# Retention and mixture of experts on one core: later pairs' q loaded by heads, GpSimd's scalings and the early counts reordered

## The chip, the cores and the metric

The kernel runs on one core of a Trainium2 chip. Five engines work side by side, each with an instruction queue of its own that it executes in order: TensorE (PE; its weight loads are listed apart, as PEld), VectorE (DVE), ScalarE (ACT), GpSimd (POOL) and SyncE (SP), which here only issues DMAs. They meet at semaphores. Data moves between HBM and the on-chip memory over 16 DMA engines that all queues share. TensorE writes into PSUM, eight banks of 2 KB in each of 128 partitions.

The metric is the device time of one execution in microseconds. The time before is 455.89 us, the median of three runs (453.74 to 457.38).

## The reference

Two blocks follow each other. The first is retention with a decay for each head, for 4 batches, 8 heads, 768 tokens and a head size of 64:

```python
gamma = 1.0 - 2.0 ** (-5.0 - np.arange(H, dtype=np.float32))
...
for t in range(S):
    state = gamma[None, :, None, None] * state + np.einsum('bhd,bhe->bhde', k[:, :, t], v[:, :, t])
    y[:, :, t] = scale * np.einsum('bhd,bhde->bhe', q[:, :, t], state)
```

Its output, as 3072 rows of 512, goes through a layer of 8 experts. Each row goes to the one expert with the largest logit:

```python
logits = x @ w_gate
expert_idx = np.argmax(logits, axis=1)
...
    h = np.maximum(x_sorted[lo:hi] @ w1[e], 0.0)
    y_sorted[lo:hi] = h @ w2[e]
...
return (gate_w[:, None] * y).astype(np.float32)
```

w1 is 8 x 512 x 1024 and w2 is 8 x 1024 x 512, all in float32.

## The kernel before

**Retention in chunks.** The tokens of a batch are cut into six chunks of 128. A step `s` (0 to 11, `STEPS` is 12) handles one chunk of two batches: `where[s]` gives `m` (which 256 tokens), `b1` (which two batches) and `e` (which half of the 256). Two steps in a row, an even and an odd one, make a pair: they share one load of q, 256 tokens of two batches. Decays are folded into q and v by a table, `dec`: q is multiplied by a forward decay (`scale_q`, giving `qs`), v by a backward one (`scale_v`, giving `vs`), and the products then need no decay of their own.

In a step, TensorE computes in this order: `scores` (k against q, line 532), `with_state` (the old state against q, 555), the gate's logits of the step before (614, 623), the transposes of the next step's k (`turn_k`, 500), in odd steps the transposes of the next pair's q (`turn_q`, 500), the new state (`next_state`, 568) and `within` (masked scores against vs, 586). VectorE masks the scores (`am`, 536), adds the state (574) and turns the outputs to rows (`to_rows`, 597). ScalarE copies transposes out of PSUM (`qT`, 513; `kT`, 519) and the outputs (589, 592). SyncE issues the loads of q three steps ahead, of k three ahead and of v two ahead, and stores the rows to `x_d` in HBM, four DMAs a step (604). GpSimd does the scalings (489, 494).

**q before the change.** For each batch of a pair one DMA brings 256 tokens of all heads, two tokens to a partition, into a tile of its own (four buffers). `scale_q(s, b)` scales batch `b`: two instructions, one for the even and one for the odd tokens. `turn_q(s, b)` transposes these and two ScalarE copies interleave them into `qT2[b]`.

**Order of the work.** All five queues are written out by hand (`manual_schedule`), in the order of the loop at line 788. For GpSimd that is, in step `s`: `scale_q(s+1, 1)` if `s` is odd, then the `scale_v` that `SCALED` names (the step's own by default), then `scale_q(s+2, 0)` if `s` is even. `SCALED` gives step 8 the v of steps 8 and 9, step 9 that of step 10, and step 10 none.

**Routing beside it.** `place(i)` is a generator with the routing of steps 0 to 4, 5 to 8 and 9 to 11 (`NEXT`). `WHEN` says at which points of which steps its next portion is put into the queues. `place(1)` starts in step 9; its last portion, in step 10 after the logits' transposes, is `found` (708), `inv` (712), `sources` (184 to 187) and the gathers of the first 256 rows of experts 0 and 1, with the `scale_v` of step 11 between. It leaves a count per expert in `acc[:, 2]`. `pad_ranks` (725 to 731) then raises the counts of these two experts, so that later rows don't fill places of the gathered 256: a small matmul `tot` and three VectorE instructions. It is called in step 10 after `next_state`. `found`, `tot`, the new state and the transposes of k all take banks of the PSUM tag "tr", which has two.

**Experts.** While the last step still runs, the 256 gathered rows of expert 0 go through w1 (`hp`, 232) and w2; then the experts follow one by one, with products split in quarters and halves (311, 357) and plain ones for the rest (245). The tiles `we` reuse the bytes of q's tiles.

Of the kernel before, what the change touches and what calls it, by code (L numbers as in the profile page):

```python
# [13 lines left out]
F32 = mybir.dt.float32  # L14
# [4 lines left out]
ALU = mybir.AluOpType  # L19
AX = mybir.AxisListType  # L20

P = 128


NC = 6


def decay_table(H, D):

    gamma = 1.0 - 2.0 ** (-5.0 - np.arange(H, dtype=np.float64))
    i = np.arange(P, dtype=np.float64)[:, None]
    on = [gamma ** (2 * P * m + 2 * i + e + 1) / math.sqrt(D) for m in range(NC // 2) for e in range(2)]
    back = [gamma ** -(P * c + i + 1) for c in range(NC)]
    return np.concatenate(on + back, 1).astype(np.float32)


def inner(ap, n):

    dims = [list(d) for d in ap.ap]
    return bass.AP(tensor=ap.tensor, offset=ap.offset, ap=dims + [[0, n]])
# [9 lines left out]
def kernel(  # L54
# [11 lines left out]
    nc = tc.nc  # L66
    B, H, S, D = q.shape
# [3 lines left out]
    HP = H // 2  # L71
# [24 lines left out]
    x_d = dram.tile([N, Q * DT * L], F32, tag="x_d", name="x_d")  # L96


    dec = const.tile([P, 2 * NC * H], F32, tag="dec", name="dec")
    wg = const.tile([P, DT, P // DT], F32, tag="wg", name="wg")  # L100
    ident = const.tile([P, P], F32, tag="ident", name="ident")
    ones = const.tile([P, P], F32, tag="ones", name="ones")
# [39 lines left out]
    acc = rt([P, NR + 1, E], "acc", BF16)  # L142
# [112 lines left out]
    FH, DH = FT // 2, DM // 2  # L255
# [195 lines left out]
    with ExitStack() as actx:  # L451
        att = actx.enter_context(tc.tile_pool(name="att", bufs=2))
# [13 lines left out]
        where = [(s // 4, s // 2 % 2, s % 2) for s in range(STEPS)]  # L466
        raw, front, state, x = {}, {}, {}, {}
        lg = keep.tile([P, NT, E], F32, tag="lg", name="lg")
        qT2 = [None, None]

        def load(nm, s, b, parts=1):
            m, b1, e = where[s]
            src = {"q": q, "k": k, "v": v}[nm]
            if nm == "q":
                to = att.tile([P, H, 2 * D], F32, tag=nm, name=nm, bufs=4)
                for part in (ts(i, H // parts) for i in range(parts)):
                    nc.sync.dma_start(to[:, part, :], src[2 * b1 + b, part, ts(m, 2 * P), :].rearrange(
                        "h (t e) d -> t h (e d)", e=2))
            else:
                to = att.tile([P, H, D], F32, tag=nm, name=nm, bufs=8)  # L480
                nc.sync.dma_start(to, src[2 * b1 + b, :, ts(2 * m + e, P), :].rearrange("h t d -> t h d"))
            raw[nm, s, b] = to

        def scale_q(s, b, by=nc.gpsimd, parts=1):
            got = raw.pop(("q", s, b))
            qs = raw["qs", s, b] = att.tile([P, 2, H, D], F32, tag="qs", name="qs")
            for part in (ts(i, H // parts) for i in range(parts)):
                for e in range(2):
                    by.tensor_tensor(out=qs[:, e, part, :], in0=got[:, part, ts(e, D)], op=ALU.mult,  # L489
                                     in1=inner(dec[:, ts(2 * where[s][0] + e, H)][:, part], D))  # L490

        def scale_v(s, b, by=nc.gpsimd):
            vs = att.tile([P, H, D], F32, tag="vs", name="vs", bufs=4)
            by.tensor_tensor(out=vs, in0=raw.pop(("v", s, b)), op=ALU.mult,  # L494
                             in1=inner(dec[:, ts(NC + 2 * where[s][0] + where[s][2], H)], D))
            raw["vs", s, b] = vs

        def heads_first(src, tr, pairs=range(HP)):
# [5 lines left out]

        def turn_q(s, b, parts=1, by=(nc.scalar.copy, nc.scalar.copy)):
            qs = raw.pop(("qs", s, b))
            qT2[b] = att.tile([P, HP, P, 2], F32, tag="qT", name="qT")
            trs = [pairs_of("sc", 4, "trq") for _ in range(2)]
            for i in range(parts):
                for e in range(2):  # L510
                    heads_first(qs[:, e, :, :], trs[e], range(i * HP // parts, (i + 1) * HP // parts))
            for e in range(2):
                by[e](out=qT2[b][:, :, :, e], in_=trs[e])

        def turn_k(s, b):
            kT = att.tile([P, HP, P], F32, tag="kT", name="kT")
# [3 lines left out]
            front[s, b] = kT  # L520

        def q_of(s, b):
            return qT2[b][:, :, ts(where[s][2], P // 2), :].rearrange("p a t e -> p a (t e)")

        def scores(s, b):
            kT, qT = front.pop((s, b)), q_of(s, b)
# [103 lines left out]
        def place(i):  # L630
# [82 lines left out]
            if i == NR - 2:  # L713
                head = inv[:, :, 0 : TC + HALF]
                src, far = sources(head, "_e")
                for e in range(2):
                    gather(xs2[e], src[:, e * TC :], range(HALF), 2 * NEXT[i + 1] * P)
                    if e == 0:
                        for b in range(2):
                            scale_v(STEPS - 1, b)  # L720
                early.extend([head, far])

        def pad_ranks(at):

            tot = ps("tr", 2, "tot")[:, 0:2]
            nc.tensor.matmul(tot, lhsT=ones_b, rhs=at, start=True, stop=True)
            pad = att.tile([P, 2], F32, tag="pad", name="pad")
            nc.vector.scalar_tensor_tensor(out=pad, in0=inner(row2[:, 0], 2), scalar=float(EARLY), in1=tot,
                                           op0=ALU.add, op1=ALU.subtract)
            nc.vector.tensor_scalar(out=pad, in0=pad, scalar1=0.0, scalar2=2.0, op0=ALU.max, op1=ALU.min)  # L730
            nc.vector.tensor_tensor(out=at, in0=at, in1=pad, op=ALU.add)
# [45 lines left out]
                copies[t](out=xT[:, :, ts(t, P)], in_=tr)  # L777

        VALUES = {STEPS - 5: (STEPS - 3, STEPS - 2)}
        SCALED = {STEPS - 4: (STEPS - 4, STEPS - 3), STEPS - 3: (STEPS - 2,), STEPS - 2: ()}  # L780
        rest = iter(())
        WHEN = {5: "abc", 6: "b", 7: "ab", 8: "pp", 9: "ac", 10: "mpp"}

# [4 lines left out]
        for s in range(STEPS):  # L788
            if s + 3 < STEPS:
                if s % 2:  # L790
                    load_all("q", s + 3)
                load_all("k", s + 3)
            for i in VALUES.get(s, (s + 2,) if s + 5 < STEPS else ()):
                load_all("v", i)
            if s % 2 and s + 1 < STEPS:
                scale_q(s + 1, 1)
            for i in SCALED.get(s, (s,) if 0 < s < STEPS - 1 else ()):
                for b in range(2):
                    scale_v(i, b)
# [24 lines left out]
            if s:  # L824
                if s + 1 < STEPS:
                    logit = logits(s - 1)
                    ahead()
                if s + 1 == STEPS:
                    xe = whole_rows(xs2[0])
                reduce = logits_of(s - 1, *logit)  # L830
                step(s, "p")
                if s + 1 < STEPS:
                    ahead_q()
                to_rows(s - 1)
                reduce()
# [12 lines left out]
            step(s, "b")  # L848
            if s == NEXT[NR - 1] + 1:
                pad_ranks(acc[:, NR - 1, 0:2])  # L850
            step(s, "r")
            within(s, y, am, (lambda: early_rows(xe, xTa, (nc.vector.tensor_copy, nc.scalar.copy)))
                   if s + 1 == STEPS else lambda: None)
            step(s, "c")
# [1 line left out]
        egates, edst = gates_of(early[0], "_e"), targets(*early, "_e")  # L856
        rest = place(NR - 1)
        oa = xs2[0][:, 0:HALF, :]
        we = [att.tile([P, FH * DH], F32, tag=tag, name="we", bufs=bufs)
              for tag, bufs in [("q", 4)] * 4]  # L860


        def within_early(f):
# [260 lines left out]
```

## Time and profile before

| | |
|---|---|
| median of three runs | 455.89 us |
| the profiled execution's own time | 458.76 us |
| its span, first to last instruction | 456.8 us |
| busy: PE, PEld, DVE, ACT, POOL | 430.3, 361.4, 292.1, 131.9, 260.5 us |
| mean granted clock of TensorE | 0.987 |
| share of the chain that ended last: PE, DMA, DVE | 75%, 7%, 7% |
| DMA share over the first 12 of 40 slices | 0.8 to 0.9 or more |
| DMA packets, bytes | 94471, 72.75 MB |

The span is what the profiler saw of the engines; about 2.0 us lie around it in the execution's own time. Retention takes about the first 126 us, the experts the rest. A busy TensorE is not TensorE at its peak: matmuls are pipelined and their ends are modelled. Three groups of the page belong to the change:

| group | count | mean ns |
|---|---|---|
| POOL qs (489), 128x512 | 22 | 1042 |
| POOL vs (494), 128x512 | 23 | 1045 |
| SyncE loads of q (477), 512 KB | 11 | lands 6.1 us after issue |

In a view's line, "idle before <- releaser" in square brackets is the time for which the engine had stood still and what ended that wait.

### The profile page before, as it was taken

The page shows a single profiled execution, that of the slowest core. Times are in us where ns is not written, and L with a number is a line of the kernel's source. Part 1 is how long each engine was busy: PE and PEld are TensorE (multiplying, and loading weights), DVE is VectorE, ACT ScalarE, POOL GpSimd, SP SyncE. Part 2 cuts the span into 40 slices and gives each one's busy share as a digit, 9 for nine tenths or more (in the row PEclk, how much of TensorE's full clock was granted, in tenths as well). Part 3 has the DMA queues.
Part 4 walks back from the last instruction along what each step waited for, and adds up shares of the span by engine and source line. Part 5 has one row for each costly group of instructions (what it writes and reads, how often), then busy time and mean ns, then how long its engine had stood idle before and what let it go on. Part 6 is the DMA issues. An engine that isn't in the chain of part 4 may idle for free.

```text
span 456.8 us, 9680 instructions
## 1 busy us (share of the span) xinstructions
PE 430.3 (94%) x3651; PEld 361.4 (79%) x3651; DVE 292.1 (64%) x600; ACT 131.9 (29%) x298; POOL 260.5 (57%) x216
## 2 busy tenths in 40 slices
PE   6999998969799999999999999999899999999992
PEld 3788887858678868869968985997798689599772
DVE  4454787667868974775776678387677768744410
ACT  2356354334342112310331321124133113202310
POOL 4474544252506978519845890985489189278311
PEclk9999999989899999999999999999999999999997
DMA  8999999999966546644532815172272534001001
GB/s 190 213 236 205 229 205 219 238 214 250 304 187 230 187 120 218 250 187 128 192 99 94 279 53 183 42 292 85 110 249 74 187 101 164 6 5 64 4 29 50
DMA packets 94471, 72.75 MB, mean 159 GB/s; under 512 B 53898, under 2 KB 78474, under 8 KB 94352
## 3 DMA queue, kind: packets, MB, share of 16 engines
q1 hardware_dynamic: 89088, 58.74, 45.9%
q0 software_dynamic: 5120, 12.60, 8.2%
q8 instruction: 47, 0.77, 0.7%
q14 instruction: 72, 0.59, 0.4%
q10 hardware_dynamic: 144, 0.05, 0.0%
HBM read 60.88 MB, written 14.68 MB: 165 GB/s over the span
## 4 chain that ended last, share of the span: by engine, by line
PE 75%; DMA 7%; DVE 7%; issue 4%; SPq 3%; POOL 2%; ACT 1%; POOLq 0%; ACTq 0%; DVEq 0%
PE p L311 27%; PE p L357 17%; PE p L245 13%; DMA q<-in_q_dram 4%; PE hp L232 3%; PE y L586 3%; DMA v<-in_v_dram 3%; SPq L604 2%; PE sc L532 2%; PE p L232 2%; PE new L568 1%; PE y L555 1%; DMA w1t<-in_moe_w_dram 1%; PE yp L357 1%; POOL qs L489 1%
## 5 line engine op out<-in xcount | busy, mean ns | idle before, releaser
L245 PE MATMUL p<-w2t,hT 128*8 128x128 f32 (+6 forms) x496 | 66.4, 360 | 0.0
L245 PEld LDWEIGHTS p<-w2t,hT 128*8 128x8 f32 (+6 forms) x496 | 32.6, 123 | 29.2 <-issue 26.4
L405 POOL DMA_INDIRECT out_dram<-o,dst x30 | 29.9, 995 | 29.1 <-ACT o L253 13.0
L216 DVE STREAM_TRANSPOSE xT<-xs 32x512 f32<-32x512 f32 (+1 forms) x64 | 40.7, 635 | 6.8 <-issue 5.5
L536 DVE TENSOR_TENSOR am<-sc,causal 128x512 f32<-128x512 f32 x48 | 30.0, 683 | 21.0 <-PE sc L532 20.9
L494 POOL TENSOR_TENSOR vs<-v,dec 128x512 f32<-128x512 f32 x23 | 23.7, 1045 | 33.5 <-DMA v<-in_v_dram 33.3
L311 PE MATMUL p<-t,s 128*128 128x196 f32 (+5 forms) x224 | 41.7, 329 | 0.0
L311 PE MATMUL p<-t,w1t 128*128 128x196 f32 (+5 forms) x224 | 41.7, 329 | 0.0
L1083 POOL COPY turn_of<-t 128x1 f32<-128x1 f32 x6 | 1.1, 184 | 70.1 <-DVE t L297 70.1
L315 DVE TENSOR_TENSOR hT<-p,q 128x196 f32<-128x196 f32 (+5 forms) x84 | 28.6, 359 | 16.6 <-PE p L311 16.0
L216 DVE STREAM_TRANSPOSE xTs<-xs 32x512 f32<-32x512 f32 x48 | 33.7, 702 | 7.0 <-issue 6.1
L173 POOL DMA_INDIRECT xs<-x_d,src x28 | 29.6, 1059 | 14.8 <-issue 8.0
L311 PEld LDWEIGHTS p<-t,s 128*128 128x128 f32 x224 | 37.8, 190 | 0.0
L311 PEld LDWEIGHTS p<-t,w1t 128*128 128x128 f32 x224 | 37.8, 190 | 0.0
L357 PE MATMUL p<-ws,hs 128*128 128x256 f32 x168 | 37.4, 379 | 0.0
L315 DVE TENSOR_TENSOR q<-p,q 128x196 f32<-128x196 f32 (+5 forms) x56 | 19.0, 360 | 26.8 <-ACT q L323 13.5
L357 PEld LDWEIGHTS p<-ws,hs 128*128 128x128 f32 x168 | 31.9, 190 | 4.3
L273 POOL TENSOR_TENSOR ws<-w2t,ws 128x1024 f32<-128x1024 f32 x14 | 34.4, 2455 | 0.6
L273 POOL TENSOR_TENSOR ws<-w2t 128x1024 f32<-128x1024 f32 x14 | 33.2, 2369 | 0.1
L489 POOL TENSOR_TENSOR qs<-q,dec 128x512 f32<-128x512 f32 x22 | 22.3, 1042 | 17.0 <-DMA q<-in_q_dram 16.1
L363 DVE SCALAR_TENSOR_TENSOR o<-p,gate,q 128x256 f32<-128x256 f32 x21 | 10.0, 483 | 27.9 <-PE p L357 23.8
L357 PE MATMUL p<-w2t,hT 128*128 128x256 f32 x112 | 26.9, 381 | 0.1
(203 smaller groups left out, 835.1 us busy)
## 6 DMA issues: line engine op xcount, KB each, us to landing
w1t<-in_moe_w_dram SPq DMA_DIRECT2D x7, 2048.0 KB, 8.7
w2t<-in_moe_w_dram SPq DMA_DIRECT2D x7, 2048.0 KB, 9.4
k<-in_k_dram SPq DMA_DIRECT2D x24, 256.0 KB, 5.1
v<-in_v_dram SPq DMA_DIRECT2D x24, 256.0 KB, 5.7
x_d<-xg SPq DMA_DIRECT2D x48, 128.0 KB, 3.9
q<-in_q_dram SPq DMA_DIRECT2D x11, 512.0 KB, 6.1
w1t<-in_moe_w_dram SPq DMA_DIRECT2D x2, 1024.0 KB, 8.6
w2t<-in_moe_w_dram SPq DMA_DIRECT2D x2, 1024.0 KB, 9.8
```

The source lines that it names most:

```text
L173: nc.gpsimd.indirect_dma_start(out=xs[:, t, :], out_offset=None, in_=x_d[0:rows, :], in_offset=bass.IndirectOffsetOnAxis(ap=idx[:, t : t + ...
L216: nc.vector.transpose(xT[ts(g, L), :, 0 : n * P].rearrange("p a (t r i) -> p r t a i", r=Q, i=L)[:, r, :, :, :], xs[ts(r, L), tiles[0] : t ...
L232: nc.tensor.matmul(hp, lhsT=w1t[:, 0, dt, ts(f, P)], rhs=xT[:, dt, 0:n], start=(dt == 0), stop=(dt == DT - 1))
L245: nc.tensor.matmul(y[j * z : j * z + m, 0:c], lhsT=hT[:, f, t * P + r0 : t * P + r0 + m], rhs=w2t[:, 0, f, ts(j, c)], start=(i == 0), stop ...
L273: by.tensor_tensor(out=ws[i], in0=sums[i][0], in1=sums[i][1], op=ALU.subtract)
L311: nc.tensor.matmul(rows(y), lhsT=a(d, f), rhs=b(d), start=start and d == 0, stop=d == 1, skip_group_check=True)
L315: nc.vector.tensor_tensor(out=to, in0=rows(y), in1=rows(plus), op=ALU.add)
L357: nc.tensor.matmul(y, lhsT=a[:, f, :], rhs=b[:, f, :], start=start and f == 0, stop=f == FH - 1, skip_group_check=True)
L405: done = nc.gpsimd.indirect_dma_start(out=out[:, :], out_offset=bass.IndirectOffsetOnAxis(ap=idx[:, t : t + 1], axis=0), in_=o[:, t, :], i ...
L489: by.tensor_tensor(out=qs[:, e, part, :], in0=got[:, part, ts(e, D)], op=ALU.mult, in1=inner(dec[:, ts(2 * where[s][0] + e, H)][:, part], D))
L494: by.tensor_tensor(out=vs, in0=raw.pop(("v", s, b)), op=ALU.mult, in1=inner(dec[:, ts(NC + 2 * where[s][0] + where[s][2], H)], D))
L536: nc.vector.tensor_tensor(out=am[j], in0=sc[j], in1=middle(causal[:, :], HP), op=ALU.mult)
```

## The change

Four things change. First, from the second pair on, q comes by heads: one DMA per head brings the 256 tokens of both batches, four tokens (1024 B) to a partition, and the partitions alternate between the batches. The tile holds the pair, so there are two buffers of twice the size. The first pair keeps its layout inside the new tile. The decay table gets columns for the four tokens. Second, `scale_q(s, b)` and `turn_q(s, b)` with `b` 0 and 1 now stand for tokens 0, 1 and 2, 3 of each four, of both batches; ScalarE's copies put them in place in one tile `qT` for both batches. Third, `SCALED` leaves step 8 its own v alone and gives step 9 the v of steps 9 and 10. Fourth, `pad_ranks` moves from step 10 after `next_state` into the last portion of `place(1)`, behind the gathers.

```diff
+R = 4
+ON = 2 + R * NC // 2
...
-    on = [gamma ** (2 * P * m + 2 * i + e + 1) / math.sqrt(D) for m in range(NC // 2) for e in range(2)]
+    on = [gamma ** (2 * i + e + 1) / math.sqrt(D) for e in range(2)]
+    on += [gamma ** (2 * P * m + R * (i // 2) + r + 1) / math.sqrt(D) for m in range(NC // 2) for r in range(R)]
...
-    dec = const.tile([P, 2 * NC * H], F32, tag="dec", name="dec")
+    dec = const.tile([P, (ON + NC) * H], F32, tag="dec", name="dec")
...
             if nm == "q":
-                to = att.tile([P, H, 2 * D], F32, tag=nm, name=nm, bufs=4)
+                if (nm, s) not in raw:
+                    raw[nm, s] = att.tile([P, H, R * D], F32, tag=nm, name=nm, bufs=2)
+                if s:
+                    for h in range(b * H // 2, (b + 1) * H // 2):
+                        nc.sync.dma_start(raw[nm, s][:, h, :],
+                                          src[2 * b1 : 2 * b1 + 2, h, ts(m, 2 * P), :].rearrange(
+                                              "b (i r) d -> i b (r d)", r=R))
+                    return
                 for part in (ts(i, H // parts) for i in range(parts)):
-                    nc.sync.dma_start(to[:, part, :], src[2 * b1 + b, part, ts(m, 2 * P), :].rearrange(
+                    nc.sync.dma_start(raw[nm, s][:, part, ts(b, 2 * D)], src[2 * b1 + b, part, ts(m, 2 * P), :].rearrange(
                         "h (t e) d -> t h (e d)", e=2))
...
         def scale_q(s, b, by=nc.gpsimd, parts=1):
-            got = raw.pop(("q", s, b))
+            got = raw["q", s]
+            on = 2 + R * where[s][0] + 2 * b if s else 0
...
-                    by.tensor_tensor(out=qs[:, e, part, :], in0=got[:, part, ts(e, D)], op=ALU.mult,
-                                     in1=inner(dec[:, ts(2 * where[s][0] + e, H)][:, part], D))
+                    by.tensor_tensor(out=qs[:, e, part, :], in0=got[:, part, ts(2 * b + e, D)], op=ALU.mult,
+                                     in1=inner(dec[:, ts(on + e, H)][:, part], D))
...
-            qT2[b] = att.tile([P, HP, P, 2], F32, tag="qT", name="qT")
+            if b == 0:
+                qT2[0] = att.tile([P, HP, 2, 2 * P], F32, tag="qT", name="qT", bufs=1)
...
-                by[e](out=qT2[b][:, :, :, e], in_=trs[e])
+                if s:
+                    by[e](out=qT2[0].rearrange("p a b (i r) -> p a i b r", r=R)[:, :, :, :, 2 * b + e],
+                          in_=trs[e].rearrange("p a (i b) -> p a i b", b=2))
+                else:
+                    by[e](out=qT2[0][:, :, b, :].rearrange("p a (t e) -> p a t e", e=2)[:, :, :, e], in_=trs[e])
...
-            return qT2[b][:, :, ts(where[s][2], P // 2), :].rearrange("p a t e -> p a (t e)")
+            return qT2[0][:, :, b, ts(where[s][2], P)]
...
                         for b in range(2):
                             scale_v(STEPS - 1, b)
+                pad_ranks(acc[:, NR - 1, 0:2])
                 early.extend([head, far])
...
-        SCALED = {STEPS - 4: (STEPS - 4, STEPS - 3), STEPS - 3: (STEPS - 2,), STEPS - 2: ()}
+        SCALED = {STEPS - 3: (STEPS - 3, STEPS - 2), STEPS - 2: ()}
...
             step(s, "b")
-            if s == NEXT[NR - 1] + 1:
-                pad_ranks(acc[:, NR - 1, 0:2])
             step(s, "r")
...
-        we = [att.tile([P, FH * DH], F32, tag=tag, name="we", bufs=bufs)
-              for tag, bufs in [("q", 4)] * 4]
+        we = [x[:, i, :] for x in (att.tile([P, 2, FH * DH], F32, tag="q", name="we", bufs=2) for _ in range(2))
+              for i in range(2)]
```

More of the change, by code (lines that the diff above doesn't have):

```diff
@@ L468 @@
         lg = keep.tile([P, NT, E], F32, tag="lg", name="lg")
-        qT2 = [None, None]
+        qT2 = [None]
         def load(nm, s, b, parts=1):
@@ L474, in load @@
             if nm == "q":
[L475 removed]
+                if (nm, s) not in raw:
[6 more added lines that the diff above has]
+                    return
                 for part in (ts(i, H // parts) for i in range(parts)):
[L477 removed]
+                    nc.sync.dma_start(raw[nm, s][:, part, ts(b, 2 * D)], src[2 * b1 + b, part, ts(m, 2 * P), :].rearrange(
                         "h (t e) d -> t h (e d)", e=2))
             else:
[L480 removed]
+                to = raw[nm, s, b] = att.tile([P, H, D], F32, tag=nm, name=nm, bufs=8)
                 nc.sync.dma_start(to, src[2 * b1 + b, :, ts(2 * m + e, P), :].rearrange("h t d -> t h d"))
[L482 removed]
         def scale_q(s, b, by=nc.gpsimd, parts=1):
[L485 removed]
+            got = raw["q", s]
+            on = 2 + R * where[s][0] + 2 * b if s else 0
             qs = raw["qs", s, b] = att.tile([P, 2, H, D], F32, tag="qs", name="qs")
@@ L494, in scale_v @@
             by.tensor_tensor(out=vs, in0=raw.pop(("v", s, b)), op=ALU.mult,
-                             in1=inner(dec[:, ts(NC + 2 * where[s][0] + where[s][2], H)], D))
+                             in1=inner(dec[:, ts(ON + 2 * where[s][0] + where[s][2], H)], D))
             raw["vs", s, b] = vs
```

## The prediction

> **What bounds the kernel now.** I read the granted clock first, then the chain of waits, then each engine's timeline where the chain leaves TensorE. From 126 us on, the chain is almost only TensorE and what feeds it from inside the chip: a microsecond won before 126 is a microsecond at the end. Ahead of 126 the chain alternates between loads (q, v), GpSimd's scalings and TensorE. The change acts in that part alone. Two holes stand out there. In this view of stretches the columns after the stretch are its length, then busy time of PE, PEld, DVE, ACT, POOL, then granted clock, DMA share and GB/s:
>
> ```profile
> 96.30:99.80 3.50, 0.06 (x2) 0.02 (x1) 3.24 (x6) 0.55 (x2) 3.15 (x4) 1.00 0.97 233
> 100.10:103.50 3.40, 3.26 (x16) 2.29 (x13) 0.71 (x1) 1.83 (x3) 3.40 (x4) 0.50 0.94 224
> ...
> 117.10:119.50 2.40, 0.00 (x1) 0.01 (x1) 2.40 (x3) 0.00 (x0) 2.24 (x3) 1.00 0.89 262
> 120.60:124.00 3.40, 3.40 (x42) 2.52 (x34) 2.01 (x4) 1.08 (x3) 0.68 (x1) 0.50 0.93 277
> ```
>
> TensorE stands still for 3.5 and for 2.4 us, and after each hole its clock is 0.50 for 3.4 us. The timeline (start, length) says who makes the first hole:
>
> ```profile
> 96.65 2.08 POOL L494 TENSOR_TENSOR vs<-v,dec 128x512 f32<-128x512 f32 x2 [10.24 <-DMA v<-in_v_dram]
> ...
> 98.69 4.05 POOL L489 TENSOR_TENSOR qs<-q,dec 128x512 f32<-128x512 f32 x4
> ...
> 99.78 3.99 PE L500 MATMUL trq<-ident,qs 128*128 128x128 f32 x16 [3.44 <-POOL qs L489]
> ...
> 100.10 0.71 DVE L648 TENSOR_TENSOR ohs<-em,idx 128x64 bf16<-128x64 f32 x1
> ...
> 103.70 1.97 PE L586 MATMUL y<-am,vs 128*64 128x128 f32 x32
> ...
> 105.94 1.27 PE L532 MATMUL sc<-qT,kT 64*128 64x128 f32 x18
> ```
>
> GpSimd, in order, sits 10.24 us on v of step 9; q of step 10 landed at 89.8 and 91.7 (packet and semaphore records) and is scaled only afterwards, so TensorE's transposes `trq` wait and then go at GpSimd's pace. The second hole:
>
> ```profile
> 112.69 0.32 DVE L712 TENSOR_TENSOR inv<-inv,found 128x160 f32<-128x160 f32 x1
> ...
> 113.06 0.16 PE L726 MATMUL tot<-acc,ones_b 128*128 128x2 bf16 x1
> ...
> 114.11 1.25 POOL L173 DMA_INDIRECT xs<-x_d,src_e  x1 [7.44 <-DMA w1t<-in_moe_w_dram]
> ...
> 116.17 2.61 DVE L731 TENSOR_TENSOR acc<-acc,pad 128x2 bf16<-128x2 bf16 x1
> 116.69 2.05 POOL L494 TENSOR_TENSOR vs<-v,dec 128x512 f32<-128x512 f32 x2
> ...
> 118.70 2.47 DVE L536 TENSOR_TENSOR am<-sc,causal 128x512 f32<-128x512 f32 x4
> ...
> 119.52 0.64 PE L614 MATMUL parts<-xT,wg 128*32 128x256 f32 x8 [2.42 <-DVE am L536]
> ```
>
> A two-element addition of `pad_ranks` takes 2.61 us and ends with GpSimd's two `vs`; a like one of eight elements (L678) takes 0.17 us at 106.74, with no scaling beside it. The mask `am` and TensorE wait behind it. Finally the load queue, from the timeline of SyncE:
>
> ```profile
> 84.57 2.08 SPq L477 DMA_DIRECT2D q<-in_q_dram  x2
> ...
> 100.51 6.42 SPq L604 DMA_DIRECT2D x_d<-xg  x8
> ```
>
> SyncE issues without a pause from 0.8 to 110 us, with the DMA share near 1: v lands when the stream has got there.
>
> **GpSimd's order (the first hole).** In step 8 `scale_v(9)` goes; four `qs` of 1.04 us follow as soon as q has landed: 91.7 to 95.9, at the latest. `trq` then starts when TensorE is free, 96.35, and takes 1.9 us, as in other pairs: 98.2. `scale_v(9)` now stands behind `scale_q(10,1)`, but v lands at 96.65 anyway: vs at 97.7 and 98.7. So step 9's `y` runs 98.2 to 100.15. Next is `rk`, which needs `ohs`; VectorE ends it at 100.82 (its small steps are held up by GpSimd's scalings, which lie there after the change too, as vs of steps 9 and 10). A new wait of 0.65 us; `rk` 100.85, `sc` of step 10 at 101.2 instead of 105.94: **-4.7 us**. Queued behind the moved `scale_v(9)` are vs of step 10 (done by 100.8, needed at 107) and the `told` copies, which need VectorE's gate of 101.5: no loss.
>
> **Place of the counts (the second hole), in the old clock times.** `pad_ranks` now follows `sources` and the gathers inside `place(1)`. Its matmul `tot` comes ahead of `next_state(10)`, and both take a "tr" bank, of which there are two: kT, kT, found, tot, new. So `new` now needs the bank of `found`, which VectorE frees at 113.01. `new` goes from 111.81 to 113.06, `y` from 113.15 to 114.25, `sc` from 115.05 to 116.2: +1.15 us on TensorE, a new wait. VectorE's three small steps run at 113.85 to 114.35, before GpSimd's scalings, at 0.14, 0.17 and, for the addition, 0.17 instead of 2.61. To its other end the addition waits for the scalings again, to 118.78; the nearest row is the two-input `he` at 141.16, which took its usual 0.69 us beside a gather, so I take 0.17. Behind it: rows of step 9 (0.5 later), their store and the w2t load on SyncE's queue, which lands at 130 and is needed at 140. `am` starts when `sc` has a half, 117.3 instead of 118.7, and `parts` at 118.2 instead of 119.52: -1.3 us.
>
> The half-speed stretch is worth more. The trace gives 4.64 us from 119.52 to `tre` at 124.16; the same four groups at full clock are 0.57 + 1.03 + 0.22 + 0.90 = 2.7 us. The Trainium skill (TensorE: Matmul & The Clock Gate, Part 1) halves the clock only after an idle window of some 3.4 us; by that the 2.4 us hole would cost no clock, and its end would gain 1.3. The row shows 0.50 after 2.4 us idle, while a 1.51 us wait before 80.48 left 1.00. I go by the row: the remaining new waits (0.65, 1.2) are short, so **-3.2 us** at `tre`, then 121. The gathered rows allow it: same issue in old time, landing 119.2 and 120.2, two copies of 0.6.
>
> **q by heads.** Five pairs come as 8 DMAs of 128 KB instead of 2 of 512 KB: 40 issues for 10 on SyncE's queue, before k, v and the stores. Packets double to 1024 B. Median packets in the trace: 512 B 27 ns, 2048 B 84 ns, so 1024 B is about 46: 1024 packets on 16 engines are 2.9 us a pair, where the two halves now land 1.84 us apart, 3.7 a pair: -0.8. Issue can bind instead: four `x_d` DMAs of the same 128 KB are 0.45 to 0.50 us apart, 4.0 a pair: +0.3. The Trainium skill (DMA: Bandwidth & Descriptors, Rules for kernel authors, and its fit of 2.0 us + bytes/436 GB/s) speaks against small transfers: 2.3 us each against 3.2, +12 a pair if in sequence. The row speaks against that: `x_d` DMAs in flight together land 0.34 to 0.42 us apart. I take -0.1 a pair, **-0.5 us** for five; ends -4 and, at 0.80 us a DMA as in the x8 row above, +13.5.
>
> `scale_q(s,0)` now waits for the whole pair, 1.8 us more, with `scale_q(s,1)` and the next vs behind it. In steps 4 and 6 GpSimd then waits 1.94 and 2.17 us for v anyway; in step 2 `new` has 1.3 us to spare. Nothing; without that cover 1 us once. The twenty qT copies write in pairs of batches: no such row; contiguous ones take 0.59, those of stride two 0.63. I take 0.63; twice that is +2.5 us a pair on ScalarE, where 3.5 us lie between the last copy (79.3) and `sc` (82.85). Buffer sizes stay, `qT` in one buffer is written after its readers in TensorE's order, the larger decay table is one DMA at the start, and `we` lies in the same bytes: nothing. The first pair shares a tile: 0, at most +1.5 if its two halves are waited for together.
>
> **Sum:** -4.7 - 3.2 - 0.5 = -8.4. The profiled execution is 458.76 (span 456.8 and 2.0 around it): 450.4. It lies 2.9 above the median of the runs, 455.89; off that, **447.5**.
>
> **Rivals.** (1) The moved addition waits as long as before, now with the rows (1.3), a reduction (0.2) and the state (0.7) behind it: `am` at 121.0, both the hole and the half clock stay, +2.3 instead of -3.2, in all -2.9: **453.0**. For: the addition started in a gather's record (115.67 to 116.68) and still did not finish before vs. Against: `he`. (2) Slower: q's small DMAs hold SyncE's queue. At 0.80 us each a pair takes 6.4 instead of 3.7, v of step 9 comes 13.5 us later, -7.9 + 13.5 = +5.6: **461.5**. For: the x8 row, and that TensorE waits for v already. Against: that row lies in a full stream with two long issues (1.24 and 1.56). It decides from (7.9 / 5 + 3.7) / 8 = 0.66 us a DMA. (3) The new order does nothing, as q(10) lands as late as v(9), 96.6: then `trq` ends at 101 and `sc` starts 2 us later, 449.5; q precedes v by two k in the queue, which speaks against.
>
> **How the numbers follow.** Forecast 0.58, rival 1 0.17, rival 2 0.15, rival 3 0.05, nothing or unforeseen 0.05. The three runs spread over 3.6 us, so 1% (4.6 us: 451.3 and 460.4) is about what can be told from no change. Faster 0.63, same 0.21, slower 0.16. The range leaves out rival 2: low end 447.5 less 3.5 of loads and some spread, 443.5; high end rival 1 with 1.5 of loads and start and the same spread, 456.
>
> **What would show it.** Right: no hole at `trq` of step 9 and no 0.50 clock after it; `qs` right after q's landing and ahead of vs; `acc` by L731 at 0.2 us; `new` of step 10 waiting about 1.2 us for `inv`; one clock of 1.00 up to the end. Wrong: SyncE's issues of q above 0.66 us each and longer waits of vs for v; `acc` still at 2 us; `trq` still waiting; qT copies over 1 us.

## The result, and the profile after

The changed kernel takes 456.79 us (median of 22 runs, 454.29 to 462.83), the kernel before, on the same chip, 454.72 (22 runs, 452.26 to 460.53): ratio 1.0039, interval 1.0018 to 1.006. A later comparison gave 456.96 against 456.2, ratio 0.9979 (0.9933 to 1.0024). Within 1%, no gain can be told, where 447.5 was forecast.

Both changes of order are in the trace as described. The timeline of the changed kernel where the two holes were (start, length, engine, line, operation, what it reads and writes, count; in brackets the idle time before it and who ended it):

```profile
94.84 4.04 POOL L501 TENSOR_TENSOR qs<-q,dec 128x512 f32<-128x512 f32 x4 [6.25 <-DMA k<-in_k_dram]
98.90 1.91 PE L512 MATMUL trq<-ident,qs 128*128 128x128 f32 x16
99.03 4.13 POOL L506 TENSOR_TENSOR vs<-v,dec 128x512 f32<-128x512 f32 x4
...
103.30 0.20 PE L683 MATMUL rk<-ohs,before 128*128 128x64 bf16 x1 [0.59 <-DVE ohs L665]
...
103.63 2.06 PE L549 MATMUL sc<-qT,kT 64*128 64x128 f32 x32
...
111.34 1.15 PE L585 MATMUL new<-vs,k 128*64 128x64 f32 x32 [1.27 <-DVE inv L729]
...
112.30 0.16 DVE L749 TENSOR_TENSOR acc<-acc,pad 128x2 bf16<-128x2 bf16 x1
...
116.20 0.64 PE L631 MATMUL parts<-xT,wg 128*32 128x256 f32 x8
...
120.44 0.66 PE L794 MATMUL tre<-ident,xe 128*128 128x128 f32 x4 [1.17 <-ACT xe L786]
...
121.47 0.66 PE L794 MATMUL tre<-ident,xe 128*128 128x128 f32 x4 [0.38 <-ACT xe L786]
...
123.08 1.13 PE L237 MATMUL hp<-xTa,w1t 128*128 128x256 f32 x4
```

GpSimd scales q ahead of v, and `trq` follows at once, without a hole and at full speed (1.91 us for 16 transposes instead of 3.99). `rk` waits 0.59 us for `ohs` and `new` 1.27 for `inv`, the two new waits foreseen at 0.65 and 1.15. The addition of the counts takes 0.16 us. But `sc` of step 10 is at 103.63, foreseen at 101.2, since q itself landed late, and `tre` now waits 1.17 and 0.38 us for the gathered rows. The first layer of the early tiles, `hp`, starts at 123.08: 3.05 us earlier than in the first profile of the kernel before (126.13), and no earlier than in its second one (122.98, below).

Why q landed late stands in the answer of the trace on its line, L484:

```profile
L484 SPq DMA_DIRECT2D q<-in_q_dram x40: 547/604/1703, 10.6 to 91.3; - x40
```

and in that on the transfers from 10 to 90 us:

```profile
DMA packets 47847, 17.05 MB, mean 213 GB/s; under 512 B 37229, under 2 KB 47833, under 8 KB 47833
```

The numbers after x40 in the first are the shortest, the median and the longest of SyncE's times in ns. From one start to the next are 0.649 us, the median of the same records: at most 128 KB in 0.649 us, or 202 GB/s, while q is issued. The packets themselves are as cheap as estimated (median 46 ns for 1 KB). In the stretches view, three stretches in which they are issued (after the stretch: its length, busy time of PE, PEld, DVE, ACT, POOL, granted clock, DMA share, GB/s):

```profile
14.00:19.00 5.00, 4.70 (x80) 4.05 (x76) 1.50 (x3) 2.59 (x5) 0.00 (x0) 1.00 0.70 199
47.00:53.00 6.00, 5.83 (x118) 4.87 (x112) 3.44 (x7) 2.39 (x5) 0.99 (x1) 1.00 0.67 180
68.00:74.00 6.00, 5.83 (x102) 5.11 (x96) 3.29 (x9) 3.11 (x6) 1.47 (x2) 1.00 0.62 172
```

The same stretches of the run named "the order" below, which differs from the changed kernel in that it loads q as before, in two DMAs a pair:

```profile
14.00:19.00 5.00, 4.70 (x84) 4.05 (x82) 1.75 (x3) 2.34 (x5) 2.50 (x3) 1.00 1.23 279
47.00:53.00 6.00, 5.83 (x104) 5.01 (x102) 2.81 (x6) 3.00 (x6) 3.40 (x4) 1.00 1.24 272
68.00:74.00 6.00, 5.99 (x110) 5.12 (x107) 5.97 (x9) 2.12 (x4) 4.29 (x4) 1.00 1.09 210
```

The DMA share is 0.62 to 0.70 in the changed kernel and 1.09 to 1.24 in the order: with q by heads the DMA engines are a third idle. So I read that they wait for SyncE, not SyncE for them; the run with two queues, below, tests it.

One thing in this profile is not typical: the execution took 461.69 us, 4.9 above the median, and the difference lies at one place, ahead of expert 0:

```profile
150.70 1.97 PE L362 MATMUL yp<-w2t,he 128*128 128x256 f32 x8 [0.16 <-DVE xs L368]
157.40 10.44 PE L237 MATMUL p<-xTa,w1t 128*128 128x104 f32 x64 [4.73 <-DVE xT L221]
```

TensorE's branch into the code for expert 0's number of tokens took 5.25 us there (start 151.89 in the instruction records; 0.38 in the kernel before), and the clock after it was 0.50 for 6.8 us. The named releaser, `xT`, is not what it waited for. More on it at the end. In the executions profiled here without such a branch the time from `hp` to the end is 329.4 to 331.7 us, whatever was changed ahead of it (332.5 in one run that left work out), so `hp` tells the time: `hp` + 331 + 2. By that, this execution without the branch would have taken 123.1 + 333 = 456.1, near the median. Executions more than 1.5% above the fastest of their kernel are left out of all ratios, but not of the medians; of GpSimd's order alone, below, that leaves two of four, 450.9 and 451.5, and no ratio.

### The profile page after: what moved, and what is told of

It reads as the page before. It is cut to its first block, busy times and chain, and to the rows that moved or that the text cites. A ratio compares the mean times of both kernels' runs of the same rounds, so it can differ in the third digit from the quotient of the medians.

```text
span 459.7 us, 9725 instructions
## 1 busy us (share of the span) xinstructions
PE 431.8 (94%) x3651; PEld 363.7 (79%) x3651; DVE 287.6 (63%) x600; ACT 140.7 (31%) x298; POOL 260.7 (57%) x216
## 4 chain that ended last, share of the span: by engine, by line
PE 78%; DMA 5%; SPq 4%; issue 3%; DVE 3%; POOL 3%; ACT 2%; POOLq 0%; ACTq 0%; DVEq 0%
PE p L316 27%; PE p L362 18%; PE p L250 14%; PE y L603 3%; PE hp L237 3%; PE sc L549 3%; PE p L237 2%; DMA v<-in_v_dram 2%; PE new L585 2%; DMA xs<-x_d,src_e 1%; SPq L493 1%; POOL vs L506 1%; SPq L484 1%; POOL qs L501 1%; PE yp L362 1%
## 5 line engine op out<-in xcount | busy, mean ns | idle before, releaser
L178 POOL DMA_INDIRECT xs<-x_d,src x28 | 29.6, 1058 | 14.8 <-issue 8.3
L344 ACT ACTIVATE hT<-p 128x196 f32<-128x196 f32 (+5 forms) x28 | 9.3, 333 | 60.9 <-PE p L316 60.9
```

The costliest lines, as they stand in the source:

```text
L178: nc.gpsimd.indirect_dma_start(out=xs[:, t, :], out_offset=None, in_=x_d[0:rows, :], in_offset=bass.IndirectOffsetOnAxis(ap=idx[:, t : t + ...
```

## The experiments

In all runs "the order" is the new order of GpSimd's scalings with the new place of the counts, q loaded as before. The table has the median (runs), the ratio to the kernel before on the same chip with its interval, and from each profile the start of `hp` and the mean transfer rate from 10 to 90 us.

| kernel | us | ratio | `hp` | GB/s |
|---|---|---|---|---|
| before, second profile | 455.48 (1) | | 122.98 | 227 |
| whole change | 456.79 (22) | 1.0039 (1.0018 to 1.006) | 123.08 | 213 |
| whole change again | 456.96 (11) | 0.9979 (0.9933 to 1.0024) | 125.22 | 209 |
| the order | 452.39 (6) | 0.9919 (0.9887 to 0.9951) | 119.51 | 225 |
| the order again | 452.83 (12) | 0.992 (0.9889 to 0.9952) | 118.37 | 227 |
| GpSimd's order alone | 454.71 (4) | | 118.51 | 226 |
| counts' place alone | 457.0 (10) | 0.9999 (0.996 to 1.0038) | 120.35 | 227 |
| q by heads alone | 464.6 (4) | 1.0168 (1.013 to 1.0206) | 132.63 | 205 |
| order, old q in 8 DMAs | 454.97 (10) | 0.9956 (0.9908 to 1.0004) | 120.62 | 217 |
| whole, q in 2 DMAs to 64 partitions | 460.57 (10) | 1.01 (1.0059 to 1.0141) | 129.24 | 202 |
| whole, scaled by halves of the heads | 456.79 (10) | 1.0027 (1.0006 to 1.0049) | 126.20 | 211 |
| order, qT copies twice | 452.76 (10) | 0.9961 (0.9925 to 0.9998) | 118.69 | 228 |
| order, q's halves swapped | 450.4 (4) | 0.9897 (0.9837 to 0.9957) | 117.31 | 230 |
| the same again | 451.35 (6) | 0.9895 (0.9853 to 0.9936) | 117.20 | 230 |
| whole, q from two queues | 451.93 (10) | 0.9965 (0.9941 to 0.9988) | 120.56 | 223 |
| order, constant rows | 449.69 (4) | 0.9845 (0.9777 to 0.9914) | 117.33 | 224 |
| GpSimd's order, constant rows | 450.43 (4) | 0.9879 (0.9821 to 0.9936) | 116.22 | 223 |

**The parts one by one.** The two edits of the order, alone and together:

```diff
-        SCALED = {STEPS - 4: (STEPS - 4, STEPS - 3), STEPS - 3: (STEPS - 2,), STEPS - 2: ()}
+        SCALED = {STEPS - 3: (STEPS - 3, STEPS - 2), STEPS - 2: ()}
...
+                pad_ranks(acc[:, NR - 1, 0:2])
                 early.extend([head, far])
...
-            if s == NEXT[NR - 1] + 1:
-                pad_ranks(acc[:, NR - 1, 0:2])
```

Both:

> Only the order of GpSimd's scalings and the place of the counts are changed; q is loaded, scaled and turned as before. Theory A (the changed kernel's loss is q by heads, plus a late TensorE branch into expert 0's job, of about 5 us, that comes by chance or by the new q code): `hp` starts at 118 to 119 us (126.1 before, 123.1 after the whole change), no granted clock under 1.00 before 140, TensorE's branch ahead of expert 0 takes 0.4 us, and the time is 447 to 449 (-6 to -8 against the kernel before). Theory B (whatever wins time ahead of 126 us brings the late branch on, since the job's code is then wanted before it is there): `hp` as in A, but TensorE waits about 5 us ahead of expert 0 and the next matmuls run at half clock, time 453 to 455. Theory C (the order itself wins nothing at the end): `hp` at 123 or later.

The first edit alone:

> Only the order of GpSimd's scalings. As the prediction had it: -4.7 us ahead of `sc` of step 10, at the end -4.7, 451; the second hole and its half clock stay. Theory A: the same, 450 to 452. Theory B: the gain shows at `hp`, and TensorE's late branch eats it: 455. Theory C: 455 with no gain at `hp`.

The others alone:

> Only the place of the counts. As the prediction had it: -3.2 us at `tre`, the half clock after it gone, 452.5. Theory A: the same, 452 to 453. Rival 1 of the prediction (the addition waits as long as before): -0 to +1 at `hp`, 455 to 456. Theory B: the gain shows at `hp`, and TensorE's late branch eats it: 455.

And the whole change with both undone, that is q by heads alone:

> Only q of the later pairs by heads; GpSimd's order and the counts stay as before. Theory A: q's 40 small DMAs cost SyncE's queue about 0.5 us a pair and more, the v loads land about 2.4 us later by step 9, `hp` at 128 to 129, time 457 to 459 (+2 to +4). If the late branch belongs to the code of this part, another 5 to 6: 462 to 464. Theory B: `hp` as in A, the branch takes 0.4 us, since the pair ends later than before: 457 to 459. As the prediction had it: 455.4 (-0.5).

The order gains 0.8%, 3.5 us; q by heads alone loses 1.7%, 7.7 us (8.7 by the medians). Neither is as forecast. The whole change is some 2 to 4 us better than the sum of the two. In the profiles that difference lies ahead of the landing of v of step 9, where both kernels have the same work: q by heads alone scales this v at 102.7, the whole change at 99.0 and 100.2. From there to `hp` q by heads alone takes 29.9 us, as the kernel before does, and the whole change 24.1 and 25.0. Why the loads came later in the first was not separated. Theory B falls: `hp` at 118.4 to 120.4 brought no late branch (0.36 to 0.45 us in all these profiles). GpSimd's order alone, with 450.9 and 451.5 in the two executions left, looks worth as much as both edits together; two executions are few, but the stretches below agree. The counts' place alone is the same as before by its ratio, though `hp` is earlier in its profile; its runs spread from 453.2 to 460.6, the profile is of one of 453.47, and what the longer ones have more was not seen.

Since loads differ by up to 3 us from execution to execution, the parts are better compared from the landing of v of step 9, where GpSimd's `vs` waits for it. From there to `hp`: 29.5 and 29.6 us in the two profiles of the kernel before, 26.7 with the counts' place, 24.3 with GpSimd's order, 24.7 and 24.7 with both. So GpSimd's order is worth 5.2 to 5.3, the counts' place 2.8 to 2.9 alone, and nothing beside the other.

**Is before's first profile typical?** And the changed kernel's?

> The kernel before once more, for a second profile of it. In the first one v of step 9 landed at 96.65 us and the time was 458.8, 4 above the median of all its runs; with the same loads the run with the counts alone moved had v at 93.6. If the load stream differs from execution to execution, v of step 9 lands at 93 to 95 here, `hp` at 123 to 124, and the time is 454 to 456.

> The whole change once more, for a second profile of it. If TensorE's branch of 5.2 us ahead of expert 0 belongs to the change, it is there again. If it is chance (the parts of the change run alone showed 0.36 to 0.44 us there), it is at 0.4 us and the time is 455 to 457, with `hp` at 122 to 125.

In the second profile of the kernel before v of step 9 is scaled at 93.3 instead of 96.65, `hp` starts at 122.98 and the time is 455.48: the first profile was of an execution with late loads, and its 2.9 us over the median were rightly taken off. In the second profile of the whole change (464.44 us) the late branch is there again, at 154.6 with 5.01 us; the median of its runs, 456.96, is that of executions without.

**What in q by heads costs.** First the number of DMAs, in the old layout:

```diff
-                    load_all("q", s + 3)
+                    for b in range(2):
+                        load("q", s + 3, b, 4)
```

> The kernel before with the new order of GpSimd's scalings and the new place of the counts; q of the later pairs in its old layout (512 B packets, batch by batch), but each half loaded as 4 DMAs of 128 KB, 8 a pair. Theory D (the number of DMAs costs: SyncE needs 0.7 to 0.8 us for each, in which the queue runs dry): SyncE's time for a pair's q is 5.5 to 6.5 us, v of step 9 lands 4 to 7 us later than with two DMAs, and the time is 456 to 460 (452.4 with two DMAs a pair). Theory E (the form of the new q costs: 1 KB packets, the wait for the whole pair, qT copies in pairs of batches): 452 to 453.

The answers on q's line and on the transfers from 10 to 90 us:

```profile
L477 SPq DMA_DIRECT2D q<-in_q_dram x40: 411/468/1747, 10.7 to 89.4; - x40
```

```profile
DMA packets 52952, 17.37 MB, mean 217 GB/s; under 512 B 37219, under 2 KB 52938, under 8 KB 52938
```

Eight DMAs of the old form take SyncE 0.468 us each, 0.513 from start to start, 256 GB/s: faster than the 225 to 227 GB/s of the stream with two DMAs a pair, and still the mean rate falls to 217. `hp` comes 1.1 and 2.3 us later than in the two profiles of the order, the median 2.6 and 2.1 later than its medians; the intervals of the ratios overlap. That is a part of the loss, and less than theory D had. The new form is dearer at the same 128 KB, 0.604 against 0.468. It differs from the old one in the length of its packets and in the order of its partitions, and which of the two makes it dearer was not separated.

Then the form itself, with fewer DMAs:

```diff
-                    for h in range(b * H // 2, (b + 1) * H // 2):
-                        nc.sync.dma_start(raw[nm, s][:, h, :],
-                                          src[2 * b1 : 2 * b1 + 2, h, ts(m, 2 * P), :].rearrange(
-                                              "b (i r) d -> i b (r d)", r=R))
+                    nc.sync.dma_start(raw[nm, s][ts(b, P // 2), :, :], src[2 * b1 + b, :, ts(m, 2 * P), :].rearrange(
+                        "h (i r) d -> i h (r d)", r=R))
```

> The whole change, but with the batches one after the other on the partitions instead of alternating, so that a pair's q comes as 2 DMAs of 512 KB with 1 KB packets, each into 64 partitions; still four tokens to a partition, the pair waited for as a whole, and the qT copies from two runs of 64 tokens. Theory D: the queue is as full as before, half as many q packets; v of step 9 by 94 us, time 450 to 453. Theory E: 455 to 458, as the whole change. A third case: DMAs into 64 partitions run at half the rate, and it is slower than the whole change.

The answer on q's line, with the times from issue to landing:

```profile
L483 SPq DMA_DIRECT2D q<-in_q_dram x10: 601/631/1917, 10.8 to 91.6; - x10
...
DMA to landing us min/median/max: 5.5/7.5/9.9
```

The third case came true: SyncE is done with a pair after 1.3 to 2.6 us, but a 1 KB packet into these 64 partitions takes 84 ns instead of 46 (medians of the packet records). It says nothing against theory D, and it shows why the batches alternate on the partitions.

Next, what follows the landing. Scaling by halves of the heads (one scaling over two tokens and four heads instead of one token and eight), doubled copies, and swapped halves:

```diff
+                part = ts(b, H // 2)
+                for i in range(2):
...
+                    by.tensor_tensor(out=raw["qs", s, i][:, :, part, :], op=ALU.mult,
+                                     in0=got[:, part, ts(i, 2 * D)].rearrange("p h (e d) -> p e h d", e=2),
...
-                by[e](out=qT2[b][:, :, :, e], in_=trs[e])
+                for _ in range(2 if s else 1):
+                    by[e](out=qT2[b][:, :, :, e], in_=trs[e])
...
-                    load_all("q", s + 3)
+                    for b in (1, 0):
+                        load("q", s + 3, b)
```

> The whole change, but GpSimd scales a pair's q by halves of the heads (four heads, all four tokens of a partition) instead of by halves of the tokens, so that it starts when 4 of the 8 DMAs have landed instead of all 8; the same number of scalings of the same size. Theory F (beside the number of DMAs, the wait for the whole pair costs: GpSimd's last q scaling ends 4 us after the last landing, now 2): `hp` 2 us earlier, time 454 to 455.5 (457.0 for the whole change). Theory G (the rest of the loss is ScalarE's qT copies of 1.19 instead of 0.64 us): no gain, 456.5 to 457.5.

> The kernel before with the new order and place of the counts, and each qT copy of the later pairs run twice, 1.28 us in all where the whole change has 1.19. Theory G: ScalarE's 2.6 us more a pair delay the scores: 454 to 456 against 452.4 without. Theory F: ScalarE has that time, 452 to 453.

> The kernel before with the new order and place of the counts, and the two halves of a pair's q loaded in the opposite order, so that the first scaling waits for the whole pair (2 DMAs, old layout). Theory F: GpSimd's q scalings end about 2 us later, and the time is 453.5 to 455 against 452.4. Theory G: 452 to 453.

Both theories fall. Earlier scalings gain nothing (456.79): in that profile q's scalings end at 97.2, and v of step 9 is there only at 99.7. With 2.6 us more of ScalarE a pair the median is 0.4 us higher (1.9 by the ratios, whose intervals overlap), where the whole change lies 4.4 higher, and waiting for the whole pair is not slower but faster (450.4). GpSimd and ScalarE have cover for most of this, as the prediction said. What is left is SyncE's queue, and that was tried directly:

```diff
-                        nc.sync.dma_start(raw[nm, s][:, h, :],
+                        by = nc.scalar if h % 2 else nc.sync
+                        by.dma_start(raw[nm, s][:, h, :],
```

> The whole change, but every second of a pair's 8 q DMAs is issued by ScalarE's queue, so that SyncE issues 4 a pair. Theory H (SyncE's issue is the cost: it needs 0.605 us for a DMA of the new form and 0.65 from start to start, that is 201 GB/s, where the stream runs at 235, so that the queue runs dry five times): SyncE's time for a pair's q falls to 2.6, v of step 9 comes 3 to 4 us earlier, `hp` at 118.5 to 121, time 451.5 to 453.5 (457.0 for the whole change), though ScalarE spends 2.4 us more a pair. Theory I (the loss lies in the transfers themselves or in what follows them, not in the issue): no gain, 456 to 458; or a loss, where ScalarE's issues hold up its copies: 458 and more.

The answer on q's line, from 5 to 100 us:

```profile
L485 SPq DMA_DIRECT2D q<-in_q_dram x20: 547/604/1790, 12.1 to 86.4; - x20
L485 ACTq DMA_DIRECT2D q<-in_q_dram x16: 542/618/1603, 19.7 to 73.2; - x16
```

Same DMAs, same layout, same scalings and copies; only half of the DMAs stand in another queue. GpSimd scales the first half of v of step 9 at 93.5 and the second at 95.6, where the whole change starts at 99.0; the rate is back at 223 GB/s, `hp` at 120.56, and the time is 451.93. On its chip the kernel before has 454.34, so it is 2.4 below before, where the whole change was 0.8 and 2.1 above: 3.2 to 4.5 us came back. By the ratios, 0.9965 against 0.9979 and 1.0039, it is 0.6 to 3.4, and the first two intervals overlap. Theory H holds as far as it says that SyncE's queue is the bound, for most of the loss. Not all came back: by the medians 0.7 to 1.1 us are missing to the order, by the ratios 2, and in two of the three stretches above the DMA engines are still a quarter idle:

```profile
47.00:53.00 6.00, 5.83 (x120) 4.92 (x119) 4.17 (x8) 1.95 (x4) 1.61 (x3) 1.00 0.72 179
68.00:74.00 6.00, 5.84 (x128) 5.42 (x128) 3.54 (x10) 2.24 (x5) 0.90 (x1) 1.00 0.76 190
```

Nor does the run tell two things apart: ScalarE issues its half of a pair 6 to 13 us ahead of SyncE's half (at 71.3 and 84.1 for the last pair), so q is not only issued by two queues but in part earlier too. The stream's rate in theory H, 235, is above the means in the table, 225 to 230 with q in two DMAs. The size agrees with the rates: 80 us at 213 GB/s instead of 225 are 0.96 MB, 4.3 us of the stream, and the whole change lies 4.4 us above the order by the medians (2.7 to 5.5 by its two ratios).

**What the counts add.** `tre` waits for rows in every run with GpSimd's order. So those rows were taken from a constant:

```diff
-                               in_=xs[:, t, :].rearrange("p (q a l) -> p q a l", q=Q, l=L))
+                               in_=(idle if xs is xs2[0] else xs[:, t, :]).rearrange("p (q a l) -> p q a l", q=Q, l=L))
```

> The kernel before with the new order of GpSimd's scalings and the new place of the counts; the first two early tiles' rows (one half of expert 0's early tokens) are copied from a constant tile instead of from the gathered rows, so that part of the output is not computed; the gathers still run. Theory J (the counts' gain is capped: TensorE then waits for the gathered rows, 1.5 + 0.8 us in the run with both): without that wait `hp` comes about 2 us earlier from v of step 9 on (24.7 us before, 22.4 now), time 450 to 450.5 against 452.4. Theory K (the rows are no bound; the counts move nothing for another reason): 452 to 453.

> The kernel before with the new order of GpSimd's scalings alone, counts in the old place, and the same rows copied from a constant tile. Theory J: the 2.4 us hole ahead of the logits stays and now binds; `hp` 23.4 us after v of step 9 (24.3 with the rows), time 450.5 to 451.5, about 1 more than the run with the counts moved; more, if the hole halves the clock here. Theory K: no difference to the run with the counts moved, beyond 0.5.

`hp` comes 22.2 us after v of step 9 with the counts moved (24.7 before: -2.5) and 21.2 with them in the old place (24.3: -3.1). The cap is shown: the rows bound both. But the second half of theory J is wrong, the old place was no worse here, since the hole was not there at all. The addition L731 and GpSimd's `vs`, first with GpSimd's order and gathered rows, then with constant rows:

```profile
108.99 2.61 DVE L731 TENSOR_TENSOR acc<-acc,pad 128x2 bf16<-128x2 bf16 x1
...
109.52 2.06 POOL L494 TENSOR_TENSOR vs<-v,dec 128x512 f32<-128x512 f32 x2
```

```profile
109.85 0.16 DVE L731 TENSOR_TENSOR acc<-acc,pad 128x2 bf16<-128x2 bf16 x1
...
110.58 2.05 POOL L494 TENSOR_TENSOR vs<-v,dec 128x512 f32<-128x512 f32 x2
```

An addition that starts 0.53 us ahead of the scalings is held up to their end; one that starts 0.73 ahead is not. The three other profiles with the addition in its old place, the two of before and q by heads alone, have 0.52 to 0.55 us ahead and 2.61 to 2.62 for the addition. So what it costs there turns on some 0.2 us.

**The best version.** The swap of q's halves was run once more beside the order alone:

> The kernel before with the new order and place of the counts, and the second half of a pair's q loaded first; once more, with more runs, beside the same without the swap. It was 450.4 in four runs. If the swap itself gains, 450 to 451 again and 1 to 2 under the run without it; if that was chance, both at 452.

> The kernel before with the new order and place of the counts alone, once more on the same chip as the swap of q's halves: 451.5 to 453, ratio 0.99 to 0.995.

The swap takes 451.35 us and the order alone 452.83. Both lie under both kernels, by about 1% under the kernel before. Twice the swap came out 1.5 to 2 us lower, with v of step 9 at 92.9 in both profiles (94.8 and 93.7 without), but the intervals overlap, and why v should come earlier was not tried.

## Why the prediction was wrong

**What bounds the kernel** was read rightly: everything ahead of `hp` is carried to the end one for one (329.4 to 331.7 us after it), but for the late branch.

**GpSimd's order, -4.7.** Right where it was worked out. From the scaling of v of step 9 to `sc` of step 10 are 9.3 and 9.5 us in the two profiles of before and 4.6 with this edit alone; the hole at `trq` is gone, and `rk` waits for `ohs` as said (0.56 us there). That 5.2 to 5.3 is left at `hp` is in part luck: between `parts` and `tre` another 1.6 us are won, since the half clock after the second hole does not come, and 1.1 are lost again ahead of `hp`, 0.9 of them in a wait for the gathered rows. Neither was in the forecast; both belong to the next term.

**Place of the counts, -3.2.** The edits do what was said (`new` waits 1.27, `acc` takes 0.16), and alone they give 2.8 to 2.9. The step that failed is the sum: this term was added to the first. The 1.3 us of the hole itself are seen at `parts` (18.2 us after the scaling of v with GpSimd's order alone, 16.9 and 17.4 with both), but not at `hp`. Two assumptions of the term no longer hold once the first edit is in.

"The gathered rows allow it" does not. It took the landing from the trace of before, 119.2 for a gather issued at 114.11, 5.1 us. With GpSimd's order ScalarE could copy the rows only 7.4 to 8.0 us after the issue, at a DMA share near 1. With the holes closed, that wait is what ends last:

```profile
116.44 0.66 PE L777 MATMUL tre<-ident,xe 128*128 128x128 f32 x4 [1.49 <-ACT xe L769]
...
117.90 0.66 PE L777 MATMUL tre<-ident,xe 128*128 128x128 f32 x4 [0.81 <-ACT xe L769]
```

This is the timeline of the order without q by heads: 2.3 us of waits, as much as the hole had been.

And the half clock, 1.9 us of this term, was taken from one row. The same hole of 2.42 us, in the run with GpSimd's order alone:

```profile
109.90:112.30 2.40, 0.03 (x2) 0.00 (x0) 2.40 (x3) 0.00 (x0) 2.24 (x3) 1.00 0.95 269
112.40:115.80 3.40, 3.40 (x62) 2.44 (x62) 2.91 (x6) 0.99 (x2) 1.39 (x2) 1.00 1.02 373
```

Full clock after it, where the two profiles of before had 0.50. There was no half clock left for the counts to remove.

**q by heads, -0.5.** Wrong, and the largest error: about +4.4 in the whole change, +7.7 alone. The packets were right (46 ns), the scalings and the copies had their cover, though the copies took 1.19 us instead of the 0.63 that I took. The step that failed is "Issue can bind instead: four `x_d` DMAs of the same 128 KB are 0.45 to 0.50 us apart". The nearest row had the right size and the wrong form. SyncE needs 0.604 us for a DMA of 128 rows of 1 KB with the batches alternating, 0.649 from start to start. This is rival 2, only that it decides lower than I put it. The 0.66 us a DMA came from spreading an order gain of 7.9 over five pairs. That gain was 4.7 to 5.3, and the same sum then decides at 0.58 to 0.60. As an estimate from measured numbers, 8 DMAs at 0.649 us are 5.2 us a pair where the two large ones land in 3.7, 7.5 us for five pairs: what q by heads costs alone, and more than in the whole change. For the old form in 8 DMAs, at 0.513, it gives 2.0, where 1.1 to 2.6 were measured. The rule that was set aside, that small transfers are dear (Trainium skill, DMA: Bandwidth & Descriptors, Rules for kernel authors), had the sign right. The +12 a pair is an estimate from the page's fit, which the page gives for DMAs issued by GpSimd, not by SyncE, and it is far from the measured +0.9 to +1.5 a pair.

**The rivals.** Rival 1 (the moved addition waits as long) is out: 0.16 to 0.19 us in the new place. Rival 3 (q lands as late as v) is nearly what is seen: GpSimd waits for q until 94.84 and finds v there when it is done. But that costs none of the order's gain: `sc` of step 10 comes 4.6 us after the scaling of v of step 9, as with GpSimd's order alone.

**The sum.** For the order the stretch from v of step 9 to `hp` fell by 5 us, all of it GpSimd's; v itself was scaled 0.3 to 1.5 later in its two profiles than in the second one of before, which may be chance, and the medians fell by 3.5 and 3.1. With some 4.4 for q, +0.9 to +1.3 is left, where 2.1 and 0.8 were measured. This only shows that the numbers fit together: the 4.4 is itself the difference of two of these medians.

## What to carry to other kernels

A DMA costs the issuing queue a time of its own, which for the same 128 KB was 0.513 us in one form and 0.649 in another. Multiply it by the number of DMAs, compare with the time in which the same bytes landed before, and look for a row of the same form. Where the queue was the bound, a second issuing engine gave most of the time back here. Two gains read from two holes of one trace may be added only after asking, with the first hole closed, what ends last at the second.

## What was not expected of the hardware

**The clock works on a fixed grid.** In the clock records all half-clock stretches but the last, which ends with the kernel, are 3.41 or 6.83 us long and start a multiple of 3.413 us apart (20.48 in both profiles of before). Cut into such windows, the eighteen traces have these idle times of TensorE between 60 and 170 us: windows with 2.01 to 3.41 us idle are followed by half speed, 13 of 13; of those at full speed with 1.06 to 1.78 only two of 36 are, one with 1.28 (the order with the old q in 8 DMAs) and one with 1.55 (qT copies twice). What sets these two apart is open. The hole of 2.42 us lay in one window in the kernel before (2.36 of it) and across two with GpSimd's order alone (the grid drawn back from the last stretch gives 0.93 and 1.48). The Trainium skill (TensorE: Matmul & The Clock Gate, Part 1) has the free-running window of this length, but asks for a whole idle one; here 2.01 us, some six tenths of one, were enough. So what a hole costs in clock depended here on where it fell.

**A late branch.** TensorE's branch ahead of expert 0 took 5.25 and 5.01 us in the two profiles of the whole change and 0.36 to 0.45 in the other sixteen profiles, those with the same q code among them. By the times, most executions of the whole change don't have it. Where it is, it costs some 5 us (336.6 and 337.3 from `hp` to the end). What decides it stays open.
